# The tile order of a fused attention and convolution kernel, planned with other durations for GpSimd and with two more tile pairs on VectorE

## The chip, the core and the metric
One NeuronCore of a Trainium2 chip. The metric is the device time of one launch in microseconds, as the median of several runs. TensorE (PE) multiplies matrices into PSUM, ScalarE (ACT) and VectorE (DVE) read PSUM, GpSimd (POOL) works on SBUF alone, and SyncE (SP) issues most of the DMAs.

## What is computed
Two branches over the same input x = A_q (2048 tokens, 640 channels, bf16) are mixed by a gate per token:

```
g = sigmoid(sum(x * gate_w))
a = x * (causal_conv(kv, ssm_k) + kv * ssm_D)        # kv = shift4(A_k) * A_v, convolution by FFT of 4096
b = softmax((x @ wq) @ (x @ wk).T / sqrt(20)) @ (x @ wv) @ wo   # 32 heads of 20, one shared k and v
out = g * a + (1 - g) * b
```

The attention has 32 heads over 2048 x 2048 scores, 134 million exponentials. That is the bulk of the work off TensorE. The convolution is done with discrete Fourier transforms as matmuls: spectra of kv and of ssm_k, a complex product of the spectra, and an inverse.

## The kernel before
The attention goes by groups of four heads and 512 queries: 8 head groups x 4 query blocks are 32 groups, counted 0 to 31 (`G`). A group has 16 steps `j` of 128 keys; at each step the four heads give four score tiles of 128 keys x 512 queries, one PSUM bank each. The last group is cut into three stages of 256, 128 and 128 queries, so that the end drains quickly.

Most score tiles are made by TensorE (line 1445), turned into weights by ScalarE (line 1480), and multiplied with the values by TensorE (line 1554). ScalarE takes them in units of three tiles (tile ETA, 1536 columns) and two tiles (ETB, 1024 columns) in turn, over five banks.

For some steps two of the four tiles, a pair, don't go to ScalarE. The table `DVE_J` (line 724) lists for each group the steps with such a pair; `stream` (line 1389 on) takes those tiles out of ScalarE's list and packs the rest into units. For a pair VectorE copies each score tile from one of the two side banks to SBUF (line 1527, dW), then computes the exponential by a cubic in three instructions of 1024 columns (lines 1546, 1547 and 1549; dX, dX, ETd). TensorE then multiplies ETd with the values. There are four ETd buffers, two dW and one dX.

The sum over the keys of a group stands in bank 6. VectorE copies it out when the group closes (line 1635, acc); TensorE can't close a group before all of its pairs have been multiplied in. GpSimd then divides by the row sums (line 1652).

The convolution's matmuls (lines 1821, 1882, 1951) run on TensorE between the score and value matmuls, over the same two side banks, which VectorE empties (lines 1894, 1897, 1901, 1903). Its complex product runs on GpSimd, in `mac`: for each of 40 blocks four products, two sums and two last steps, each of 256 columns (lines 1915 to 1930).

The order of all instructions on all engines is planned when the kernel is built. `Scheduler` steps a clock of each engine forward with an assumed cost for each instruction and picks the next one by readiness, priority and due time (`pick`, `pick_pe`, `pool_may`, `place`); the lists come out fixed, with semaphores between the engines. The planner holds that a VectorE instruction marked `port` (the three wide ones of a pair among them) and a GpSimd instruction exclude each other:

```
if op.port and e == "dve":
    op.end = max(start, self.pool_until - PORTP) + op.cost
elif e == "pool":
    op.end = max(start, self.port_until - PORTD) + op.cost
```

`c_pool(n)` is 0.3 + 0.00168 n us, so `c_pool(256) - 0.045` is 0.685. Where TensorE has nothing to do, the planner puts in matmuls with zeros (line 2045).

Of the kernel before, what the change touches and what calls it, by code (L numbers as in the profile page):

```python
# [7 lines left out]
ALU = mybir.AluOpType  # L8
# [712 lines left out]
TABT = 8.0  # L721
TABR = 12.5
STAGES = ((0, 256, 6), (256, 128, 5), (384, 128, 6))
DVE_J = ((), (3, 7), (2, 4, 7, 8, 11), (1, 4, 14), (1, 3, 13), (1, 7, 8, 11), (1, 2, 6, 9), (9, 13), (1, 4, 5, 6, 10, 14), (1, 4, 11), (2, 7, 9), (1, 4, 7, 14), (1, 2, 5, 6, 11), (2, 3, 8, 10), (2, 5, 6, 8), (2, 5, 6, 13), (1, 2, 5), (7, 10, 11, 13), (1, 2, 5, 12), (1, 3, 8, 13), (1, 8, 11), (1, 7, 8, 14), (3, 4, 12), (3, 9, 10, 14), (4, 9, 14), (3, 10), (2, 3, 6, 11, 13, 14), (1, 2, 9, 11), (2, 3, 6), (1, 2, 5, 6, 9), (1, 2, 9, 10, 13), (2, 5))
KIND = {}
SCALE = float(DH) ** -0.5
CK = SCALE * LOG2E * 128.0
# [34 lines left out]
def c_pool(n):  # L762
    return 0.3 + 1.68e-3 * n
# [6 lines left out]
class Kernel:  # L770
# [618 lines left out]
    def stream(self):  # L1389
# [4 lines left out]
        for G in range(LASTG + len(STAGES)):  # L1394
            for j in range(NSC if G < LASTG else NSC * STAGES[G - LASTG][1] // 512):
                mine = order
                if G <= LASTG and j in DVE_J[G]:
                    mine, rest = order[:2], order[2:]
# [11 lines left out]
    def attention(self):  # L1410
# [148 lines left out]
        def PV(G, j, rs, more=False):  # L1559
# [19 lines left out]
            if j == 0 and G <= LASTG:  # L1579
                for jd in DVE_J[G]:  # L1580
                    pe = self.ndexp % NED
# [326 lines left out]
    def mac(self, c, fc, p, prio):  # L1908

        T = self.T  # L1910
        X, K, P = T[f"X{p}"], T[f"K{p}"], T["Pp"]
        AB = T[f"AB{c % 2}"]

        def tt(out, a, b, alu, reads, writes, n, cost=None):
            f = lambda e: e.tensor_tensor(out, a, b, alu)  # L1915
            self.pool(f, reads, writes, cost or c_pool(n) - 0.045, prio=prio, port=True, name="mac")

        sh = [128, 2, 2, CW]
        sl = 2 + (NF * c + fc) % NP1
        both = slice(1, sl + 1, sl - 1)  # L1920
        for h, o in ((1, 0), (0, 1)):
            for x in range(2):
                tt(P[:, o, x, :, :], X[:, x, :].unsqueeze(1).to_broadcast([128, 2, CW]), K[:, h, :, :], ALU.mult,
                   [("X", p), ("K", p)], [("Pp", o)], 256)
        for x in range(2):
            tt(P[:, sl, x, :, :], P[:, sl, x, :, :], P[:, 0, x, :, :], ALU.add, [("Pp", sl), ("Pp", 0)], [("Pp", sl)], 256, 0.73)
        rd = [("Pp", 1), ("Pp", sl)]
        ab = [("AB%d" % (c % 2), fc)]
        tt(AB[:, fc, :, 0, :], P[:, both, 0, 0, :], P[:, both, 1, 1, :], ALU.subtract, rd, ab, 256)
        tt(AB[:, fc, :, 1, :], P[:, both, 0, 1, :], P[:, both, 1, 0, :], ALU.add, rd, ab, 256)  # L1930
        if fc == 0:

            for x in range(2):
                self.dve(lambda e, x=x: e.tensor_scalar(AB[0:1, fc, :, x, :], P[0:1, both, x, x, :], 0.5, None, ALU.mult), rd, ab, 0.19,
                         prio=prio, port=True, name="row0")
# [169 lines left out]
```

## Time and profile before
| | |
|---|---|
| median of 3 runs | 847.73 us (847.66 to 847.99) |
| the profiled execution | 848.0 us, of which the span from first to last instruction is 846.1 |
| ScalarE busy | 835.8 us, 99% |
| TensorE busy | 824.6 us, 97% |
| VectorE busy | 779.6 us, 92% |
| GpSimd busy | 328.6 us, 39% |
| granted TensorE clock | 1.0 throughout |

Durations of neighbouring instructions on ScalarE, VectorE and GpSimd overlap in the records, since one begins before the last results of the one before have landed. What an instruction costs its engine is read from start to start in a stretch without idle time, not from its duration.

### The profile page before, as it was taken

Reading aid. Unit: us, or ns where it says so; the run is one execution under the profiler, and the core shown is the slowest. Engines: PE = TensorE matmul, PEld = TensorE weight load, DVE = VectorE, ACT = ScalarE, POOL = GpSimd, SP = SyncE. Lnnn points to the kernel's source line nnn. Section 1 sums busy time; section 2 is a strip of 40 time slices with the busy share of each in tenths; the row PEclk is TensorE's granted clock in tenths of the full one; section 3 lists DMA queues with packets and bytes.
Section 4 is the critical chain, followed back from the end, with each engine's and each line's share of the span. In section 5 each row is a group of like instructions: output and inputs, shape, how many; then the busy total and the mean of one; then the engine's idle time right before and its main releaser. Section 6 shows DMA issues by size and latency. Waiting matters only on the chain.

```text
span 846.1 us, 18750 instructions
## 1 busy us (share of the span) xinstructions
PE 824.6 (97%) x7934; PEld 346.5 (41%) x7934; DVE 779.6 (92%) x1057; ACT 835.8 (99%) x748; POOL 328.6 (39%) x418
## 2 busy tenths in 40 slices
PE   8999999999999999999999999999999999999997
PEld 4234433444334444434434344444444443433334
DVE  7788999999999999999999979999989978999995
ACT  8999999999999999999999999999999999999997
POOL 3246102644555344444432653345555444301010
PEclk9999999999999999999999999999999999999999
DMA  7740022001220000200012010000200000422011
GB/s 209 188 114 14 15 57 71 21 14 16 63 59 21 14 17 12 46 20 22 15 37 54 23 44 21 17 7 19 45 21 21 14 2 15 115 69 69 32 41 43
DMA packets 55764, 36.31 MB, mean 43 GB/s; under 512 B 33059, under 2 KB 51712, under 8 KB 55680
## 3 DMA queue, kind: packets, MB, share of 16 engines
q1 hardware_dynamic: 55104, 34.90, 15.6%
q8 instruction: 62, 1.02, 0.5%
q10 hardware_dynamic: 576, 0.22, 0.1%
q14 instruction: 22, 0.18, 0.1%
HBM read 20.31 MB, written 8.51 MB: 34 GB/s over the span
## 4 chain that ended last, share of the span: by engine, by line
ACT 86%; PE 7%; DVE 5%; DMA 1%; SPq 0%; issue 0%
ACT ETA L1480 51%; ACT ETB L1480 35%; PE ps L1445 2%; PE ps L1882 2%; PE ps L1554 1%; DVE dW L1527 1%; DVE dX L1546 1%; DVE dX L1547 1%; DVE ETd L1549 1%; PE ps L1951 1%; DMA xn<-in_A_q_dram 1%; PE ps L1347 0%; PE ps L2045 0%; SPq L795 0%; PE ps L1176 0%
## 5 line engine op out<-in xcount | busy, mean ns | idle before, releaser
L1480 ACT ACTIVATE ETA<-ps 128x1536 bf16<-128x1536 f32 x364 | 573.8, 1576 | 0.8 <-PE ps L1445 0.6
L1480 ACT ACTIVATE ETB<-ps 128x1024 bf16<-128x1024 f32 x363 | 419.6, 1156 | 0.0
L1445 PE MATMUL ps<-qT,kT 32*128 32x512 bf16 (+2 forms) x2176 | 298.5, 371 | 11.1 <-ACT ETA L1480 5.2
L1527 DVE COPY dW<-ps 128x512 f32<-128x512 f32 x230 | 157.0, 684 | 21.9 <-PE ps L1445 19.8
L1915 POOL TENSOR_TENSOR Pp<-X,K 128x256 f32<-128x256 bf16 x160 | 120.0, 758 | 147.3 <-DVE ETd L1549 42.0
L1445 PEld LDWEIGHTS ps<-qT,kT 32*128 32x128 bf16 x2176 | 77.0, 91 | 227.5 <-ACT ETB L1480 111.0
L1554 PE MATMUL ps<-ETA,vaug 128*32 128x512 bf16 (+2 forms) x1168 | 152.8, 370 | 0.0
L1549 DVE SCALAR_TENSOR_TENSOR ETd<-dX,dW 128x1024 int16<-128x1024 f32 x115 | 151.2, 1315 | 0.5
L1547 DVE SCALAR_TENSOR_TENSOR dX<-dX,dW 128x1024 f32<-128x1024 f32 x115 | 149.0, 1296 | 0.6
L1546 DVE SCALAR_TENSOR_TENSOR dX<-dW 128x1024 f32<-128x1024 uint16 x115 | 148.3, 1289 | 1.3
L1554 PE MATMUL ps<-ETB,vaug 128*32 128x512 bf16 (+2 forms) x774 | 146.9, 371 | 0.8 <-ACT ETA L1480 0.7
L1951 PE MATMUL ps<-AB,Tcs 128*128 128x256 bf16 x600 | 90.2, 275 | 0.1
L1882 PE MATMUL ps<-ssm_kT,Tcs 128*128 128x256 bf16 x600 | 90.1, 275 | 0.0
L1882 PE MATMUL ps<-kv,Tcs 128*128 128x256 bf16 x600 | 87.7, 275 | 1.1 <-DVE dW L1527 1.0
L1915 POOL TENSOR_TENSOR AB<-Pp 128x256 bf16<-128x256 f32 x80 | 58.2, 727 | 77.0 <-DVE dX L1546 24.8
L1915 POOL TENSOR_TENSOR Pp<-Pp 128x256 f32<-128x256 f32 x80 | 60.9, 761 | 56.1 <-DVE dX L1547 26.2
L1652 POOL TENSOR_TENSOR oTn<-acc,rbc 128x512 bf16<-128x512 f32 x24 | 40.9, 1703 | 78.1 <-DVE xT L1359 29.2
L1951 PEld LDWEIGHTS ps<-AB,Tcs 128*128 128x128 bf16 x600 | 50.8, 98 | 35.9 <-issue 29.3
L1882 PEld LDWEIGHTS ps<-kv,Tcs 128*128 128x128 bf16 x600 | 49.1, 97 | 39.0 <-issue 25.5
L1882 PEld LDWEIGHTS ps<-ssm_kT,Tcs 128*128 128x128 bf16 x600 | 50.4, 98 | 35.1 <-issue 25.5
L2045 PE MATMUL ps<-Tcs,zeros 128*32 128x512 bf16 (+1 forms) x740 | 62.8, 381 | 1.2 <-DVE acc L1635 1.1
L1652 POOL TENSOR_TENSOR oT<-acc,rbc 128x512 bf16<-128x512 f32 x7 | 10.7, 1532 | 89.4 <-DVE outsb L1984 33.3
(174 smaller groups left out, 644.0 us busy)
## 6 DMA issues: line engine op xcount, KB each, us to landing
rbc<-scr_d SPq DMA_DIRECT2D x31, 256.0 KB
scr_o<-oTn SPq DMA_DIRECT2D x24, 128.0 KB, 1.7
kv<-in_A_v_dram SPq DMA_DIRECT2D x4, 640.0 KB
out_dram<-outsb SPq DMA_DIRECT2D x15, 160.0 KB
xn<-in_A_q_dram SPq DMA_DIRECT2D x3, 640.0 KB
scr_q<-xT SPq DMA_DIRECT2D x15, 128.0 KB, 1.8
qT<-scr_q SPq DMA_DIRECT2D x12, 160.0 KB
oTp<-scr_o SPq DMA_DIRECT2D x12, 160.0 KB, 3.0
```

What stands on the lines that cost most here:

```text
L1445: return e.matmul(self.bank(bk, n, n * t), T["kT0" if first(G, jt) else "kT4"][32 * r:32 * r + 32, 128 * jt:128 * jt + 128], T[k][32 * r:3 ...
L1480: op("act", lambda e: e.activation(et(n)[:, 0:w], self.ps[:, lo:lo + w], ACT.Exp, scale=OCT, bias=-K0 * OCT), [("ps", base[n % 2] + k) for ...
L1527: self.evac(gr, "dve", lambda e, bk, c=c: e.tensor_copy(W[:, c], self.bank(bk)), (), [kW], n).due = G
L1546: V(lambda e: e.scalar_tensor_tensor(X, w, DP, w, ALU.add, ALU.mult), [kW], ["dX"], c_dve(1024), **k).due = G
L1547: self.mid = V(lambda e: e.scalar_tensor_tensor(X, X, DQ, w, ALU.add, ALU.mult), [kW, "dX"], ["dX"], c_dve(1024), **k)
L1549: V(lambda e: e.scalar_tensor_tensor(E, X, DA, W, ALU.mult, ALU.add), [kW, "dX"], [("ETd", pe, 0), ("ETd", pe, 1)], c_dve(1024), **k).due = G
L1554: return op("pe", lambda e: e.matmul(self.bank(b, n)[32 * r:32 * r + 32, :], T[va][:, j, :], src, start=(j == 0 or cut and j == 4 * EARLY) ...
L1652: self.pool(lambda e: e.tensor_tensor(out, T["acc"][:, :], T["rbc"][:, :], ALU.mult), ["acc", "rbc"], [key], 1.27, prio=p, port=True, name ...
L1882: self.mm(gr, lambda e, bk, lhs=lhs, rhs=rhs, comp=comp, n=n: e.matmul(self.bank(bk, 256, 256 * comp), lhs, rhs, start=(n == 0), stop=(n = ...
L1915: f = lambda e: e.tensor_tensor(out, a, b, alu)
L1951: self.mm(gr, lambda e, bk, lhs=lhs, fc=fc, comp=comp, h=h: e.matmul(self.bank(bk, 256, 256 * h), lhs, AB[:, fc, :, comp, :], start=(fc == ...
L2045: sch.filler, *sch.filler2 = ([[lambda e, r=r, st=st, b=b, n=n: e.matmul(self.bank(b, n)[32 * r:32 * r + 32, :], self.T["zeros"][:, 0:32], ...
```

## The change
Two things are changed. `DVE_J` is a new table: 117 pairs in place of 115, and most steps are other ones. And in `mac` the planner's costs of GpSimd's 256-column instructions are 0.63 us for a product (0.685 before), 0.68 for a sum (0.73 before) and 0.685 for a last step (as before). No instruction on GpSimd is added, removed or altered; the costs are used by the planner alone, and so change the order.

```diff
-DVE_J = ((), (3, 7), (2, 4, 7, 8, 11), (1, 4, 14), (1, 3, 13), (1, 7, 8, 11), (1, 2, 6, 9), (9, 13), (1, 4, 5, 6, 10, 14), (1, 4, 11), (2, 7, 9), (1, 4, 7, 14), (1, 2, 5, 6, 11), (2, 3, 8, 10), (2, 5, 6, 8), (2, 5, 6, 13), (1, 2, 5), (7, 10, 11, 13), (1, 2, 5, 12), (1, 3, 8, 13), (1, 8, 11), (1, 7, 8, 14), (3, 4, 12), (3, 9, 10, 14), (4, 9, 14), (3, 10), (2, 3, 6, 11, 13, 14), (1, 2, 9, 11), (2, 3, 6), (1, 2, 5, 6, 9), (1, 2, 9, 10, 13), (2, 5))
+DVE_J = ((), (1, 11), (5, 10, 11, 14), (2, 8, 13, 14), (4, 7, 9), (3, 11, 14), (1, 2, 3, 7), (7, 8), (2, 7, 9, 12, 14), (2, 4, 10, 13, 14), (1, 7, 8, 12), (2, 7, 14), (4, 8, 10, 14), (2, 8, 11), (3, 5, 6, 8, 9, 12), (1, 3, 4), (5, 10, 12), (1, 7, 9, 13), (1, 2, 4, 14), (2, 6, 9, 14), (8, 12, 13, 14), (3, 4, 7), (3, 4, 8, 12), (3, 4, 9, 13), (1, 2, 8, 10), (1, 8, 10, 14), (4, 9, 12, 14), (1, 6, 8, 11, 13), (5, 9), (1, 3, 4, 8, 10, 11), (1, 3, 13, 14), (1, 2, 6))
...
-            self.pool(f, reads, writes, cost or c_pool(n) - 0.045, prio=prio, port=True, name="mac")
+            self.pool(f, reads, writes, cost or 0.63, prio=prio, port=True, name="mac")
...
-            tt(P[:, sl, x, :, :], P[:, sl, x, :, :], P[:, 0, x, :, :], ALU.add, [("Pp", sl), ("Pp", 0)], [("Pp", sl)], 256, 0.73)
+            tt(P[:, sl, x, :, :], P[:, sl, x, :, :], P[:, 0, x, :, :], ALU.add, [("Pp", sl), ("Pp", 0)], [("Pp", sl)], 256, 0.68)
...
-        tt(AB[:, fc, :, 0, :], P[:, both, 0, 0, :], P[:, both, 1, 1, :], ALU.subtract, rd, ab, 256)
-        tt(AB[:, fc, :, 1, :], P[:, both, 0, 1, :], P[:, both, 1, 0, :], ALU.add, rd, ab, 256)
+        tt(AB[:, fc, :, 0, :], P[:, both, 0, 0, :], P[:, both, 1, 1, :], ALU.subtract, rd, ab, 256, 0.685)
+        tt(AB[:, fc, :, 1, :], P[:, both, 0, 1, :], P[:, both, 1, 0, :], ALU.add, rd, ab, 256, 0.685)
```

## Rows read from the trace of the kernel before
The windows of rows 5 from 612 us on end where VectorE copies out the sums of groups 23 to 27.

**Rows 1.** Page, busy us, share and instructions of each engine.
```profile
PE 824.6 (97%) x7934; PEld 346.5 (41%) x7934; DVE 779.6 (92%) x1057; ACT 835.8 (99%) x748; POOL 328.6 (39%) x418
```

**Rows 2.** Timeline of ScalarE: start us, us, engine, line, operation, tiles.
```profile
16.39 1.45 ACT L1480 ACTIVATE ETA<-ps 128x1536 bf16<-128x1536 f32 x1
...
34.81 1.60 ACT L1480 ACTIVATE ETA<-ps 128x1536 bf16<-128x1536 f32 x1
36.14 1.18 ACT L1480 ACTIVATE ETB<-ps 128x1024 bf16<-128x1024 f32 x1
37.04 1.62 ACT L1480 ACTIVATE ETA<-ps 128x1536 bf16<-128x1536 f32 x1
...
838.96 1.70 ACT L1480 ACTIVATE ETA<-ps 128x1536 bf16<-128x1536 f32 x1
```

**Rows 3.** Page, costliest groups: the exponentials; busy us, mean ns, idle before.
```profile
L1480 ACT ACTIVATE ETA<-ps 128x1536 bf16<-128x1536 f32 x364 | 573.8, 1576 | 0.8 <-PE ps L1445 0.6
L1480 ACT ACTIVATE ETB<-ps 128x1024 bf16<-128x1024 f32 x363 | 419.6, 1156 | 0.0
```

**Rows 4.** Timeline around a stall of ScalarE; idle before and releaser in brackets.
```profile
248.83 1.14 ACT L1480 ACTIVATE ETB<-ps 128x1024 bf16<-128x1024 f32 x1
...
249.64 0.28 PE L1882 MATMUL ps<-kv,Tcs 128*128 128x256 bf16 x1 [0.70 <-DVE dW L1527]
...
250.34 1.45 ACT L1480 ACTIVATE ETA<-ps 128x1536 bf16<-128x1536 f32 x1 [0.38 <-PE ps L1445]
```

**Rows 5.** Windows: length; busy PE, PEld, DVE, ACT, POOL; clock, DMA.
```profile
150.00:250.00 100.00, 97.22 (x869) 38.86 (x866) 98.08 (x139) 99.96 (x89) 50.29 (x62) 1.00 0.16 36
...
612.00:638.70 26.70, 26.61 (x242) 11.49 (x241) 23.31 (x33) 26.70 (x25) 13.56 (x20) 1.00 0.06 17
638.70:664.50 25.80, 25.66 (x248) 10.58 (x247) 23.86 (x31) 25.80 (x24) 13.51 (x19) 1.00 0.06 17
664.50:691.50 27.00, 27.00 (x252) 11.79 (x252) 21.27 (x27) 27.00 (x25) 14.46 (x21) 1.00 0.04 12
691.50:715.40 23.90, 23.44 (x231) 9.74 (x230) 21.90 (x25) 23.90 (x22) 9.36 (x13) 1.00 0.04 12
715.40:740.20 24.80, 24.06 (x229) 9.59 (x228) 22.92 (x27) 24.80 (x23) 8.84 (x13) 1.00 0.40 99
```

**Rows 6.** Waits of VectorE from 612 to 740.2: us, times, longest.
```profile
DVE dW L1527 <- PE ps L1445: 10.8, 12, 2.7
```

**Rows 7.** Timeline of VectorE while GpSimd is still.
```profile
107.86 1.21 DVE L1547 SCALAR_TENSOR_TENSOR dX<-dX,dW 128x1024 f32<-128x1024 f32 x1
109.00 0.68 DVE L1527 COPY dW<-ps 128x512 f32<-128x512 f32 x1
109.60 0.68 DVE L1825 TENSOR_TENSOR kv<-ps,kv 128x512 bf16<-128x512 f32 x1
```

**Rows 8.** Page, costliest groups: the wide instructions of the pairs.
```profile
L1549 DVE SCALAR_TENSOR_TENSOR ETd<-dX,dW 128x1024 int16<-128x1024 f32 x115 | 151.2, 1315 | 0.5
L1547 DVE SCALAR_TENSOR_TENSOR dX<-dX,dW 128x1024 f32<-128x1024 f32 x115 | 149.0, 1296 | 0.6
L1546 DVE SCALAR_TENSOR_TENSOR dX<-dW 128x1024 f32<-128x1024 uint16 x115 | 148.3, 1289 | 1.3
```

**Rows 9.** Windows from 0 of line 1549 alone, the last step of a pair.
```profile
0.00:691.50 691.50, 121.97 (x92) 1.00 0.16 41
...
0.00:740.20 740.20, 133.08 (x100) 1.00 0.16 42
```

**Rows 10.** Timeline of GpSimd in a run of products and sums.
```profile
354.36 0.67 POOL L1915 TENSOR_TENSOR Pp<-X,K 128x256 f32<-128x256 bf16 x1
354.99 0.73 POOL L1915 TENSOR_TENSOR Pp<-Pp 128x256 f32<-128x256 f32 x1
```

**Rows 11.** Page, costliest groups: score matmuls, and matmuls with zeros.
```profile
L1445 PE MATMUL ps<-qT,kT 32*128 32x512 bf16 (+2 forms) x2176 | 298.5, 371 | 11.1 <-ACT ETA L1480 5.2
...
L2045 PE MATMUL ps<-Tcs,zeros 128*32 128x512 bf16 (+1 forms) x740 | 62.8, 381 | 1.2 <-DVE acc L1635 1.1
```

## The prediction
> **What bounds the kernel now.** The first view is the page's line of busy times [rows 1]: ScalarE is busy 835.8 of 846.1 us, TensorE 824.6, VectorE 779.6, GpSimd 328.6. Three engines are nearly full, so the busy share alone doesn't name the bound. The second view is ScalarE's own order in time [rows 2]. An exponential over three tiles starts at 34.81, the next over two tiles at 36.14, the next over three at 37.04: each starts where the one before lets go, and five tiles cost 2.23 us (1.33 + 0.90). The first of these instructions starts at 16.39 and the last at 838.96; in between lie 363 such pairs of instructions (364 of three tiles, 363 of two [rows 3]). 363 x 2.23 is 809.5, the stretch is 822.6: ScalarE does nothing else for 97% of the span and loses only some 13 us in it, spread thin. So the time is set by how many tiles ScalarE has to do, plus these 13 us.
>
> The third view shows how one of the larger losses arises [rows 4]: a two-tile exponential starts at 248.83, the next instruction only at 250.34, that is 1.51 after it and not 0.90. ScalarE waited for a score matmul. TensorE, which runs its list in order, stood 0.70 us in front of a spectrum matmul whose bank VectorE had not yet emptied. A late VectorE reaches ScalarE through TensorE's order; the price here was 0.61 us.
>
> The fourth view is VectorE by stretch [rows 5]. From 150 to 250 us it is busy 98.08 of 100: no room for another pair. From 612.00 to 740.20 it idles 3.39 + 1.94 + 5.73 + 2.00 + 1.88 = 14.9 us, and of its idle time there 10.8 us, in 12 waits, is spent in front of the copy that opens a pair, until TensorE has made the scores [rows 6].
>
> **The change, part by part.** *Fewer tiles on ScalarE.* Each pair takes two score tiles from ScalarE to VectorE. The table of pairs sums to 117 and not 115, so ScalarE has 1814 tiles in place of 1818. 1818 is 363 x 5 + 3; 1814 is 362 x 5 + 4, which ends with a three-tile and a one-tile instruction. By [rows 2] a tile is the difference of the two kinds, 1.33 - 0.90 = 0.43, and the fixed part 0.90 - 2 x 0.43 = 0.04. The stream loses one round of 2.23 and gains a one-tile instruction of 0.43 + 0.04 = 0.47 behind the last three-tile one: -1.76 us. All of it is on the path that sets the end.
>
> *More work on VectorE.* A pair is two copies and three 1024-column instructions. From start to start a copy takes 0.60 (109.00 to 109.60) and a wide one 1.14 (107.86 to 109.00) [rows 7]: 2 x 0.60 + 3 x 1.14 = 4.62 us, 9.24 for two pairs. To that comes what the wide ones lose to GpSimd: their means are 1289, 1296 and 1315 ns [rows 8] against 1.21 where GpSimd is still [rows 7], so 0.27 us a pair and 0.5 for two. The sum is 9.8 us of VectorE. On the path it is nothing if idle time takes it. Where does it fall? Added up group by group, the new table stands at or below the old through group 23, but for one pair after group 10 (85 in both after 23), then at 93 against 90 after group 25, 102 against 100 after group 27, and 117 against 115 at the end. VectorE works a little ahead of its table: when groups 25 and 27 close, at 691.50 and 740.20, it has finished 92 and 100 pairs [rows 9], so it must have one more and two more by then. So the full stretch gets no more work, and the two pairs have to be absorbed between about 612 and 740 us, where the idle time is 14.9 us against the 9.8 needed. It fits, with 5 us left in 128. I take 0 for this edit. The bounds: at worst only the idle time that isn't a wait for scores can be used, 14.9 - 10.8 = 4.1 us, and 9.8 - 4.1 = 5.7 us come late; at best a VectorE whose pairs sit better removes a few stalls, below.
>
> What [rows 8] show of GpSimd is that the wide instructions last longer on average than alone, while none is stopped for good. The Trainium skill (SBUF — State Buffer, "Who interferes with whom") says that VectorE instructions with two SBUF inputs and GpSimd instructions that read SBUF exclude each other through a lock, the later one blocked fully until the first ends. If each of the six added wide instructions met a whole GpSimd instruction of 0.67 us [rows 10], that would be 4.0 us in place of 0.5, and the sum 13.3 of the 14.9: still room, but next to none. The trace agrees that they hinder each other, but its 0.27 us a pair is a small share of that.
>
> *The planner's new GpSimd durations.* 160 products are entered at 0.63 and not 0.685, 80 sums at 0.68 and not 0.73; the 80 last steps keep 0.685. The trace has one product starting at 354.36 and the next instruction at 354.99, 0.63 later [rows 10], so the new figure is what the chip does. GpSimd's instructions are the same, so nothing is saved there directly: the plan held 160 x 0.055 + 80 x 0.05 = 12.8 us of GpSimd time that the chip never used, and let VectorE wait for part of it. That is why the chip's VectorE runs ahead of its list and stands in front of scores. The correction lets the plan spend this. What it may cost is the spare time itself: plan and chip now agree, and whatever the plan still has wrong meets less cover.
>
> *TensorE.* The number of score and value matmuls stays. Four tiles change from the shared score rounds to single ones that ride beside others; at worst each stands alone for 0.37 us [rows 11], 1.5 in all. I take 0: TensorE's list contains 62.8 us of dummy matmuls that are put in only where there is nothing else to do [rows 11].
>
> *All pairs placed anew.* Which of ScalarE's stalls go and which come cannot be read from the diff. The 13 us are the frame: none can gain more. Single large ones like that of [rows 4] cost 0.61; I take no change, and a spread of 1.2 us to either side, two of them.
>
> Sum: -1.76. The profiled execution took 848.0 us (span 846.1 and 1.9 around it), which makes 846.2; the median of the runs is 847.73, 0.27 less, so 846.0.
>
> **The rivals.**
> 1. *The stalls shrink too.* For it: orders now planned with durations that the chip keeps, so fewer waits in the wrong place. Against: the old figures erred on the long side, and an engine that is early makes few stalls. With a sixth of the 13 us gone as well, -1.76 - 2.1: 843.9.
> 2. *The saving is eaten.* Two or three new stalls of 0.61, since VectorE keeps 5 us of spare time where it had 14.9: 846.0 + 1.5 = 847.5, no change. For it: in the stretch with 98% busy [rows 5] lies the stall of [rows 4].
> 3. *VectorE becomes the bound in groups 24 to 27.* It cannot use its waits for scores, because these come when TensorE's list has them, and TensorE's list is tied to ScalarE. Then 5.7 us come late at the sums that close those groups, ScalarE waits for TensorE behind them, and the time is 847.73 + 5.7 - 1.76 = 851.7. It decides as soon as less than 9.8 - 1.76 = 8.0 us of the 14.9 can be filled. Against it: the waits exist because the old table had no earlier pair to give there, and the new one has.
> 4. *The change doesn't do what it says*: the order that the corrected durations give is, on the chip, no better matched than the old one, and ScalarE waits for TensorE as much longer (1.8 us of 13 would do) as it computes less: 847.7. Against it: the new durations are the chip's own.
>
> **How the numbers follow.** The forecast of 846.0 (its own range 844.8 to 847.2) has a chance of 0.48, rival 1 0.20, rivals 2 and 4 together 0.20, rival 3 0.12. What a measurement can tell from no change is about 0.2%, 1.7 us: under 846.0 counts as faster, over 849.4 as slower. The forecast lies right at that edge. Just over half of its chance (0.28) and all of rival 1 are faster: 0.48. The rest of the forecast (0.20) and rivals 2 and 4 are the same: 0.40. Rival 3 is slower: 0.12. The range reaches from a little beyond rival 1, 843.3, to part of the way into rival 3, 849.2; about 1 in 10 is left out on either side.
>
> **What would show it.** In the trace after: 363 three-tile and 362 two-tile exponentials with a one-tile one at the end, ScalarE's stretch from first to last shorter by 0.9 us (the last one starts a whole round earlier and one three-tile instruction later), and the same 1.33 and 0.90 between starts. VectorE's idle time from 612 to 740 falls from 14.9 to about 5, its waits for scores with it, while 150 to 250 stays near 98%. GpSimd's product still takes 0.63. Rival 1 would show as a stretch shortened by more than that; rival 2 as some further gaps of half a microsecond on ScalarE after 640 us; rival 3 as gaps on ScalarE near 715 and 740 released by TensorE behind VectorE. The forecast is wrong if ScalarE's losses move from 13 us by more than 1.2.

## The result, and the profile after

The kernel after takes 850.82 us (median of 6 runs, 850.58 to 851.75), the kernel before 847.86 beside it: a ratio of 1.0035, 95% interval [1.0022, 1.0048]. It is slower by 3 us, where 1.7 faster was forecast, and 1.6 us above the range. Run again (e11) it took 850.65, a ratio of 1.0034 [1.0022, 1.0047].

The page of after: span, busy times, the chain that ended last by engine, and the costliest groups that answer to [rows 3, 8] and to the complex product on GpSimd.
```profile
span 849.2 us, 18930 instructions
...
PE 824.7 (97%) x8007; PEld 348.9 (41%) x8018; DVE 789.1 (93%) x1067; ACT 836.8 (99%) x747; POOL 342.3 (40%) x418
...
ACT 51%; PE 25%; DVE 21%; issue 1%; DMA 1%; POOL 0%; SPq 0%
...
L1915 POOL TENSOR_TENSOR Pp<-X,K 128x256 f32<-128x256 bf16 x160 | 117.8, 743 | 147.6 <-DVE dX L1547 41.1
...
L1915 POOL TENSOR_TENSOR AB<-Pp 128x256 bf16<-128x256 f32 x80 | 69.8, 872 | 84.9 <-DVE dX L1546 33.7
...
L1915 POOL TENSOR_TENSOR Pp<-Pp 128x256 f32<-128x256 f32 x80 | 65.0, 812 | 40.6 <-DVE dX L1546 18.4
```

The same lines of before's page, as far as they weren't shown.
```profile
ACT 86%; PE 7%; DVE 5%; DMA 1%; SPq 0%; issue 0%
...
L1915 POOL TENSOR_TENSOR Pp<-X,K 128x256 f32<-128x256 bf16 x160 | 120.0, 758 | 147.3 <-DVE ETd L1549 42.0
...
L1915 POOL TENSOR_TENSOR AB<-Pp 128x256 bf16<-128x256 f32 x80 | 58.2, 727 | 77.0 <-DVE dX L1546 24.8
L1915 POOL TENSOR_TENSOR Pp<-Pp 128x256 f32<-128x256 f32 x80 | 60.9, 761 | 56.1 <-DVE dX L1547 26.2
```
Two things stand out. The chain runs through TensorE and VectorE for 46%, where it had run through ScalarE for 86%. And GpSimd, whose 320 instructions of the product are the same ones, is busy 13.7 us longer than in [rows 1]: the last steps take 872 ns on average and not 727, the sums 812 and not 761, while the products take 743 and not 758.

The timeline of ScalarE in after, first and last exponentials; they answer to [rows 2].
```profile
16.30 1.45 ACT L1480 ACTIVATE ETA<-ps 128x1536 bf16<-128x1536 f32 x1
...
840.96 1.51 ACT L1480 ACTIVATE ETA<-ps 128x1536 bf16<-128x1536 f32 x1
842.29 0.67 ACT L1480 ACTIVATE ETB<-ps 128x512 bf16<-128x512 f32 x1
```
From these starts the loss of ScalarE can be counted, which is used from here on: the time from the first start to the last, less what the rounds between them take at the smallest round that the traces show, 1.33 + 0.903 = 2.233 us. With 115 pairs that floor is 363 x 2.233 = 810.6, with 117 it is 362 x 2.233 + 1.33 = 809.7. Before loses 838.96 - 16.39 - 810.6 = 12.0 us, after 842.29 - 16.30 - 809.7 = 16.3. So the last start comes 3.33 us later: 4.3 from more loss, less 0.9 of floor and less 0.1 because the first start is earlier. Behind it the end takes 849.2 - 842.29 = 6.9 us, and 7.1 in before. The whole result is in the 4.3 us. They lie in many small gaps, none over 0.56 us: 2.7 of them from 150 to 450 us, 2.1 from 600 to 750, 0.7 after 800, and a little less loss than before elsewhere.

The windows of VectorE's full stretch and of the one with idle time, in after (columns as in [rows 5]), and then VectorE's waits from 612 to 740.
```profile
150.00:250.00 100.00, 97.81 (x878) 41.17 (x879) 96.94 (x135) 99.51 (x88) 51.10 (x64) 1.00 0.13 37
612.00:740.00 128.00, 123.84 (x1185) 52.27 (x1187) 119.86 (x141) 127.72 (x114) 65.24 (x75) 1.00 0.13 35
```
```profile
DVE dW L1527 <- PE ps L1445: 5.3, 6, 1.3
```
VectorE's idle time there falls from 14.9 us [rows 5] to 128 - 119.9 = 8.1 and its waits for scores from 10.8 [rows 6] to 5.3: the two pairs did go mostly where the prediction put them. Half of the new loss arises elsewhere.

### The profile page after: what moved, and what is told of

Its sections match the earlier page's. It is cut to its first block, busy times and chain, and to the rows that moved or that the text cites. A ratio compares the mean times of both kernels' runs of the same rounds, so it can differ in the third digit from the quotient of the medians.

```text
span 849.2 us, 18930 instructions
## 1 busy us (share of the span) xinstructions
PE 824.7 (97%) x8007; PEld 348.9 (41%) x8018; DVE 789.1 (93%) x1067; ACT 836.8 (99%) x747; POOL 342.3 (40%) x418
## 4 chain that ended last, share of the span: by engine, by line
ACT 51%; PE 25%; DVE 21%; issue 1%; DMA 1%; POOL 0%; SPq 0%
ACT ETA L1480 31%; ACT ETB L1480 20%; PE ps L1445 8%; PE ps L1882 6%; DVE dX L1546 5%; DVE dW L1527 4%; PE ps L1554 4%; DVE dX L1547 4%; DVE ETd L1549 4%; PE ps L1951 3%; PE ps L2045 1%; DVE Pp L1897 1%; DMA xn<-in_A_q_dram 1%; DVE acc L1635 1%; PE ps L1694 1%
## 5 line engine op out<-in xcount | busy, mean ns | idle before, releaser
L1480 ACT ACTIVATE ETA<-ps 128x1536 bf16<-128x1536 f32 x363 | 556.6, 1533 | 2.1 <-PE ps L1445 1.1
L1480 ACT ACTIVATE ETB<-ps 128x1024 bf16<-128x1024 f32 x363 | 403.6, 1112 | 0.2 <-PE ps L1445 0.2
L1527 DVE COPY dW<-ps 128x512 f32<-128x512 f32 x234 | 159.8, 683 | 19.5 <-PE ps L1445 18.2
L1915 POOL TENSOR_TENSOR Pp<-X,K 128x256 f32<-128x256 bf16 x160 | 117.8, 743 | 147.6 <-DVE dX L1547 41.1
L1546 DVE SCALAR_TENSOR_TENSOR dX<-dW 128x1024 f32<-128x1024 uint16 x117 | 154.2, 1318 | 1.4
L1547 DVE SCALAR_TENSOR_TENSOR dX<-dX,dW 128x1024 f32<-128x1024 f32 x117 | 151.8, 1298 | 0.6
L1915 POOL TENSOR_TENSOR AB<-Pp 128x256 bf16<-128x256 f32 x80 | 69.8, 872 | 84.9 <-DVE dX L1546 33.7
L1882 PE MATMUL ps<-ssm_kT,Tcs 128*128 128x256 bf16 x600 | 87.8, 274 | 0.4 <-DVE kv L1961 0.2
L1915 POOL TENSOR_TENSOR Pp<-Pp 128x256 f32<-128x256 f32 x80 | 65.0, 812 | 40.6 <-DVE dX L1546 18.4
L2045 PE MATMUL ps<-Tcs,zeros 128*32 128x512 bf16 (+2 forms) x824 | 70.7, 380 | 1.1 <-DVE acc L1635 0.8
```

The costliest lines, as they stand in the source:

```text
L1480: op("act", lambda e: e.activation(et(n)[:, 0:w], self.ps[:, lo:lo + w], ACT.Exp, scale=OCT, bias=-K0 * OCT), [("ps", base[n % 2] + k) for ...
L1527: self.evac(gr, "dve", lambda e, bk, c=c: e.tensor_copy(W[:, c], self.bank(bk)), (), [kW], n).due = G
L1546: V(lambda e: e.scalar_tensor_tensor(X, w, DP, w, ALU.add, ALU.mult), [kW], ["dX"], c_dve(1024), **k).due = G
L1547: self.mid = V(lambda e: e.scalar_tensor_tensor(X, X, DQ, w, ALU.add, ALU.mult), [kW, "dX"], ["dX"], c_dve(1024), **k)
L1882: self.mm(gr, lambda e, bk, lhs=lhs, rhs=rhs, comp=comp, n=n: e.matmul(self.bank(bk, 256, 256 * comp), lhs, rhs, start=(n == 0), stop=(n = ...
L2045: sch.filler, *sch.filler2 = ([[lambda e, r=r, st=st, b=b, n=n: e.matmul(self.bank(b, n)[32 * r:32 * r + 32, :], self.T["zeros"][:, 0:32], ...
```

## What happens on GpSimd

The timelines of VectorE and of GpSimd in after, around 650 us.
```profile
648.86 1.27 DVE L1549 SCALAR_TENSOR_TENSOR ETd<-dX,dW 128x1024 int16<-128x1024 f32 x1
650.05 0.68 DVE L1527 COPY dW<-ps 128x512 f32<-128x512 f32 x1
650.65 0.24 DVE L1645 RECIPROCAL rcp<-den 128x16 f32<-128x16 f32 x1
650.81 1.18 DVE L1546 SCALAR_TENSOR_TENSOR dX<-dW 128x1024 f32<-128x1024 uint16 x1
652.06 0.69 DVE L1527 COPY dW<-ps 128x512 f32<-128x512 f32 x1
```
```profile
648.32 0.72 POOL L1915 TENSOR_TENSOR Pp<-Pp 128x256 f32<-128x256 f32 x1
650.21 0.67 POOL L1915 TENSOR_TENSOR Pp<-X,K 128x256 f32<-128x256 bf16 x1 [1.16 <-DVE ETd L1549]
650.84 1.74 POOL L1915 TENSOR_TENSOR Pp<-Pp 128x256 f32<-128x256 f32 x1
```
GpSimd's product waits for the wide instruction that started at 648.86. That one's record ends at 650.13; VectorE has begun its next at 650.05, and GpSimd begins at 650.21: 0.08 us after the record's end, 0.16 after VectorE's next start. After has 163 such waits, and the 0.08 is 78 to 81 ns in all of them; in before it is so in 171 of 173. The product then takes its 0.63, so the sum comes at 650.84. But a wide instruction has begun at 650.81. The sum, 0.03 us too late, lasts 1.74 us where its like took 0.72 at 648.32. A race lost by 0.03 us holds GpSimd for a whole microsecond. Of the 320 instructions those over 0.8 us are 14 in before and 30 in after. In 24 of the 30 the record of GpSimd's instruction begins between 0.25 us behind and 0.05 us ahead of the start of a wide one; in before it is so in 8 of 14.

How a long GpSimd instruction reaches ScalarE is seen in the chain of waits of after (start, us, what).
```profile
157.48 1.15 DVE dX L1546
158.62 0.07 issue
158.69 2.24 POOL AB L1915
160.93 0.02 issue
160.96 0.28 DVE AB L1934
161.24 1.14 DVE ETd L1549
162.38 0.04 issue
162.43 0.39 PE ps L1554 x2
...
164.32 1.45 ACT ETA L1480
```
A last step of the product takes 2.24 us; VectorE's small instruction on its result waits for it, the last step of a pair waits behind that in VectorE's order, TensorE's value matmul waits for the pair, and ScalarE for the scores behind it. But this last step lost no race of the kind above, as the timelines of VectorE and GpSimd show.
```profile
158.53 0.67 DVE L1365 TENSOR_SCALAR cr<-ps 32x512 int16<-32x512 int32 x1
159.13 1.20 DVE L1547 SCALAR_TENSOR_TENSOR dX<-dX,dW 128x1024 f32<-128x1024 f32 x1
```
```profile
158.69 2.23 POOL L1915 TENSOR_TENSOR AB<-Pp 128x256 bf16<-128x256 f32 x1 [3.85 <-DVE dX L1546]
```
It begins 0.44 us ahead of the wide instruction and 0.16 behind an instruction of line 1365, which the planner doesn't mark `port`. Two of after's 30 long ones stand behind that line, and three of before's 14, so this kind was there before the change.

The planner doesn't know GpSimd's start. Where `place` ties a GpSimd instruction to a VectorE one (`op.deps.add(d[-2])`), the plan lets it begin as soon as the other ends. From a product's start it then lets VectorE's next wide instruction begin after the product's cost less `PORTP` (0.05): 0.685 - 0.05 = 0.635 us in before, 0.63 - 0.05 = 0.58 in after. On the chip the wide one, counted back 1.13 us from VectorE's next start, effectively begins 0.54 after the product's start (the median of 44 such cases in after); that is within 0.58, but the product may itself start 0.16 late, and 0.54 + 0.16 = 0.70 is more than either. By that reading the old surplus was no idle time: it paid for most of a start that the plan doesn't have. This is the theory (A). Its rivals: (B) the two pairs' load leaves too little spare time, whatever the durations; (C) these are just two placings of the pairs, and any other would differ as much.

## The experiments

All in one table first; "allowed" is the plan's cost of a product less `PORTP`. Medians are over all runs of a kernel, each ratio against runs of before beside it; the loss and the number of long instructions come from one profiled run each. Those of e1 and e7 were 0.4 and 0.7 us faster than their medians, those of e10 and e12 1.1 slower; the two of after's order (after and e11) lose 16.3 and 16.0. So differences in loss of some tenths carry little.

| kernel | pairs | allowed, us | median us | ratio to before [95%] | loss us | GpSimd over 0.8 us |
|---|---|---|---|---|---|---|
| before | 115 | 0.635 | 847.86 | | 12.0 | 14 |
| after | 117 | 0.58 | 850.82 | 1.0035 [1.0022, 1.0048] | 16.3 | 30 |
| e1 | 115 | 0.58 | 849.61 | 1.002 [1.0011, 1.0029] | 13.7 | 14 |
| e2 | 115, other table | 0.635 | 847.83 | 1.0 [0.9991, 1.0008] | 11.8 | 13 |
| e7 | 117, other table | 0.58 | 849.47 | 1.0017 [1.0008, 1.0027] | 14.7 | 16 |
| e8 | 117, other table | 0.62 | 848.2 | 1.0 [0.9991, 1.0009] | 14.0 | 15 |
| e9 | 117, other table | 0.635 | 850.62 | 1.003 [1.0018, 1.0041] | 13.4 | 26 |
| e10 | 116 | 0.66 | 848.18 | 1.0003 [0.9994, 1.0012] | 12.3 | 10 |
| e11 | after again | 0.58 | 850.65 | 1.0034 [1.0022, 1.0047] | 16.0 | 30 |
| e12 | 115, other table | 0.66 | 847.36 | 0.999 [0.9981, 0.9999] | 10.9 | 4 |
| e3 | order of after, product left out | | 845.51 | 0.9971 [0.996, 0.9982] | 10.9 | |
| e4 | order of before, product left out | | 846.53 | 0.9982 [0.9973, 0.9991] | 10.6 | |
| e5 | order of after, 232 columns | | 846.33 | 0.9979 [0.997, 0.9988] | 11.5 | |
| e6 | order of before, 232 columns | | 846.74 | 0.9984 [0.9976, 0.9993] | 10.8 | |

**e1, the durations alone, and e2, a new placing alone.** e1 is after with 115 pairs, before's table through group 6 and then placed for the new durations. e2 is before with another table of 115.
```diff
-DVE_J = ((), (1, 11), (5, 10, 11, 14), (2, 8, 13, 14), (4, 7, 9), (3, 11, 14),
...
+DVE_J = ((), (3, 7), (2, 4, 7, 8, 11), (1, 4, 14), (1, 3, 13), (1, 7, 8, 11),
...
```
```diff
-DVE_J = ((), (3, 7), (2, 4, 7, 8, 11), (1, 4, 14), (1, 3, 13), (1, 7, 8, 11),
...
+DVE_J = ((), (3, 5), (3, 4, 8, 13), (5, 7, 14), (2, 7, 8, 9, 12, 13), (),
...
```


> The new GpSimd costs alone: 115 pairs as before, and the table of before kept through group 6 and refitted after it only so that the planner, with the new costs, again sees ScalarE without stalls. Theory A (the padding of the old costs had paid for what the planner leaves out when the port passes between VectorE and GpSimd, so VectorE and GpSimd now come late against the list): slower than before, 849.5 to 852 us, with more GpSimd instructions of over 0.8 us than the 14 among the 320 of line 1915 before. Theory B (the two added pairs are too much for VectorE, the costs are harmless): 847.9 within 1 us.

> The old costs and 115 pairs, but another table, found from a scrambled start so that the planner sees ScalarE without stalls. Theory A and theory B: 847.9 within 1 us. Theory C (any table other than the old one loses a few us on the chip, whatever the costs): 849.5 us or more.

e1 takes 849.61 and loses 13.7 us, e2 847.83 and 11.8. The new durations alone, with no pair more, cost 1.6 us; a wholly new table for the old durations costs nothing. That is for A and against B and C as the only cause, though each stands on one table, and e1's table differs from before's behind group 6. One thing was missed: e1 has no more GpSimd instructions over 0.8 us than before, so the long ones alone are not the measure of what a short plan costs. Nor is the chain. By engine, on the pages of e1 and then of e2, it turns away from ScalarE in both, and e2 lost nothing:
```profile
ACT 62%; DVE 22%; PE 14%; issue 1%; DMA 1%; SPq 0%
...
ACT 67%; DVE 16%; PE 14%; DMA 1%; issue 1%; SPq 0%; POOL 0%
```

**e3 and e4, no contention.** The orders of after and of before, with each of the 320 instructions as a write alone.
```diff
-            f = lambda e: e.tensor_tensor(out, a, b, alu)
+            f = lambda e: e.memset(out, 0.0)
```


> The changed kernel with its order untouched, but the 320 instructions of GpSimd's complex product replaced by writes of zero that read nothing (the product is left out). Theory A: GpSimd no longer holds VectorE or is held, the losses of ScalarE fall from 16 to 12 us or less and the time to 846.5 or less. Theory C (the order on TensorE and in the banks is worse in itself): the time stays near 850 us.

> The same in the kernel before. Theory A: it gains less than the changed kernel does, under 2 us, to 846 to 847.5 us, since its plan had cover; the changed kernel without the product is then at or below this one. Theory C: the gap of 3 us between the two remains.

The wide instructions and the products of e3, on its page:
```profile
L1547 DVE SCALAR_TENSOR_TENSOR dX<-dX,dW 128x1024 f32<-128x1024 f32 x117 | 144.3, 1234 | 0.7
L1549 DVE SCALAR_TENSOR_TENSOR ETd<-dX,dW 128x1024 int16<-128x1024 f32 x117 | 144.4, 1234 | 0.2
...
L1546 DVE SCALAR_TENSOR_TENSOR dX<-dW 128x1024 f32<-128x1024 uint16 x117 | 142.8, 1221 | 1.4
L1915 POOL MEMSET Pp<- 128x256 f32 x240 | 73.7, 311 | 283.4 <-DVE dX L1546 76.5
```
The wide ones take 1.22 to 1.23 us, close to the 1.21 of [rows 7]. After's order is now the faster, 845.51 against 846.53, and the two lose about the same (10.9 and 10.6). So the order of after is not bad in itself: 1.0 of the forecast 1.76 us shows. What undoes it is GpSimd: of the 4.3 us that after loses more than before, 0.3 are left. The edit takes away two things at once, the contention and more than half of each instruction's length (311 ns); e5 separates them.

The Trainium skill (SBUF — State Buffer, "Who interferes with whom") says that a VectorE instruction with two SBUF inputs contends with a GpSimd instruction that reads SBUF and not with one that only writes it. The trace of e3 agrees: 311 ns for each write, and wide instructions nearly as short as alone. It also says ("SBUF: two separate sides") that whichever of the two starts first gets the shared ports for its whole instruction and blocks the other; the sum at 650.84 above, 1.74 us for 0.72, agrees with that. The other way the trace shows less than a whole one: the wide instruction effectively begins 0.54 us into a product that takes 0.63.

**e5 and e6, the contention kept, GpSimd slightly shorter.** Each of the 320 instructions has 232 columns in place of 256, in both orders; the inverse transform reads columns that are written, and VectorE's small instruction on the product is cut to 64 columns.
```diff
+            h = CW - 12
+            out, a, b = out[..., 0:h], a[..., 0:h], b[..., 0:h]
             f = lambda e: e.tensor_tensor(out, a, b, alu)
...
```


> The changed kernel, its order untouched; GpSimd's 320 instructions work on 232 of the 256 columns (the rest of the product is left out, and the inverse transform reads 64 columns of it twice), so that each is some 0.05 us shorter than the plan has it: the padding put back, on the chip and not in the plan. Theory A: ScalarE's losses fall from 16 to 12 or 13 us and the time to 846 to 848 us. Theory B (too many pairs): 320 x 0.05 is only 16 us less of GpSimd, VectorE has as many pairs as before, the time stays at 850 or above.

> The same shortening in the kernel before, as the control. Theory A: its plan has the padding already, so more of it gains under 1 us: 847 to 848 us.

The GpSimd groups of e5, on its page:
```profile
L1917 POOL TENSOR_TENSOR Pp<-X,K 128x232 f32<-128x232 bf16 x160 | 106.1, 669 | 156.9 <-DVE dX L1547 43.1
...
L1917 POOL TENSOR_TENSOR AB<-Pp 128x232 bf16<-128x232 f32 x80 | 60.5, 756 | 91.3 <-DVE dX L1546 37.7
L1917 POOL TENSOR_TENSOR Pp<-Pp 128x232 f32<-128x232 f32 x80 | 59.0, 737 | 44.2 <-DVE dX L1546 19.9
```
The means fall by 743 - 669 = 74 ns, 116 and 75, which is some 0.04 us of the instructions' own length (a product that isn't held records 0.63 and not 0.67) and, for the rest, shorter holds. That gives after 4.5 us (850.82 to 846.33) and before 1.3 (848.0, measured beside it, to 846.74, where under 1 was expected), and turns the order of the two round by 0.4 us. The order stays as planned with the new durations, GpSimd is given back about what the plan had taken away, and the new order loses 11.5 and not 16.3. With e3 this shows where the loss sits: between GpSimd and VectorE, in the new order. It doesn't part A from B, because VectorE is relieved too: its busy time falls from 789.1 to 779.7 us in e5 and from 779.6 to 770.9 in e6.

**e7, a second table of 117** for the new durations.
```diff
-DVE_J = ((), (1, 11), (5, 10, 11, 14), (2, 8, 13, 14), (4, 7, 9), (3, 11, 14),
...
+DVE_J = ((), (3, 11), (1, 5, 11), (4, 9, 10, 12, 14), (5, 12), (1, 2, 14),
...
```


> The new costs and 117 pairs with another table, found from a scrambled start so that the planner sees ScalarE without stalls. Theory A: it loses like the changed kernel, 849.5 to 852 us. Theory C (the table of the change was bad luck): 847 us or less.

849.47, 1.3 us less than after, with 16 long GpSimd instructions and not 30. So C holds a part: between two tables of 117 lie 1.3 us. Both are slower than before. But 1.45 of e7's 14.7 us of loss lie in one stall at 350 us. ScalarE there, and then the matmul ahead of its scores:
```profile
348.84 1.05 ACT L1480 ACTIVATE ETB<-ps 128x1024 bf16<-128x1024 f32 x1
351.19 1.45 ACT L1480 ACTIVATE ETA<-ps 128x1536 bf16<-128x1536 f32 x1 [1.30 <-PE ps L1445]
```
```profile
350.43 0.28 PE L1882 MATMUL ps<-ssm_kT,Tcs 128*128 128x256 bf16 x1 [1.30 <-DMA ssm_kT<-in_A_ssm_k_dram]
```
TensorE waited for a load of ssm_k, not for VectorE or GpSimd. Without this stall e7 loses 13.3, 3.0 less than after and no more than e1 with its 115 pairs.

**e8, 117 pairs and a hand-over nearer to the chip's.** `PORTP` is what the plan takes off after GpSimd, `PORTD` what it takes off after VectorE.
```diff
-PORTP = 0.05
-PORTD = 0.14
+PORTP = 0.01
+PORTD = 0.055
...
```


> The new costs and 117 pairs, but the planner's two allowances for passing the port are set by the traces as well: after a product VectorE's wide instruction begins 0.62 us after GpSimd's start, which with a cost of 0.63 is an allowance of 0.01 and not 0.05; and a held GpSimd instruction gets 0.055 and not 0.14 of overlap. Table refitted. Theory A: ScalarE's losses are back at 12 or 13 us and the saving of the two pairs shows: 845.5 to 847 us, below the kernel before. Theory B: 850 us or more, since VectorE has the same pairs.

A correction to that text: the 0.62 us that it gives from GpSimd's start to VectorE's wide instruction was counted back from the recorded end; from start to start, as planned, it is 0.54. So the edit didn't set the chip's hand-over; its table apart, it gave 0.04 us of padding after GpSimd and, with `PORTD`, 0.085 after VectorE. The result is 848.2, level with before, 1.3 us below e7 and 2.6 below after, but not below before as A had expected; the loss is 14.0, not 12 or 13. And the table is a third one of 117: two tables alone differ by 1.3 us, so how much of the gain is the padding's isn't shown.

**e9, the two pairs alone:** before's durations, a table of 117.
```diff
-DVE_J = ((), (3, 7), (2, 4, 7, 8, 11), (1, 4, 14), (1, 3, 13), (1, 7, 8, 11),
...
+DVE_J = ((), (8, 10), (9, 10, 11, 13), (6, 9, 10), (3, 5, 7, 12), (3, 4, 14),
...
```


> The old costs with 117 pairs, table refitted (the planner sees ScalarE without large stalls, but with the old costs it leaves VectorE's last work some 2 us later at the end than in the kernel before). Theory A: ScalarE's stream loses 12 to 13 us as before, its last instruction starts 1 to 2 us earlier than in the kernel before, and the time is 847 to 848.5 us because of the end. Theory B: the stream loses 14 us or more, and the time is 849.5 us or above.

850.62: A had expected 847 to 848.5 us and a last start 1 to 2 us earlier, and missed. The loss is 13.4, 1.4 above before, and the last start, at 839.18, is 0.2 us later than before's, so the stream gains nothing; then the end takes 848.9 - 839.2 = 9.7 us, 2.8 more than in after. VectorE's last two instructions in e9:
```profile
843.54 0.54 DVE L1748 SCALAR_TENSOR_TENSOR outsb<-ps,omgf,part 128x320 bf16<-128x320 f32 x1
845.71 0.88 DVE L1782 SCALAR_TENSOR_TENSOR outsb<-ps,omgf,part 128x640 bf16<-128x640 f32 x1 [1.63 <-PE ps L1724]
```
The last output, which starts 3.7 us after the last exponential in after (846.02), starts 6.5 us after it here, after 1.63 us of waiting for TensorE's output matmul. So e9 bears on B only up to 839: two pairs more cost 1.4 us of loss with the old durations, where they save 0.9 of floor. That is again one table. The late end is this plan's own.

**e10, 116 pairs, and e12, 115, padded.** The products' 0.63 stays and the plan adds 0.03 where it took 0.05 off; after VectorE it takes 0.055 off and not 0.14, as in e8. In e12 this holds only from the start of the main stream on.
```diff
-                op.end = max(start, self.pool_until - PORTP) + op.cost
+                op.end = max(start, self.pool_until - (-0.03 if self.main_started else PORTP)) + op.cost
...
-                op.end = max(start, self.port_until - PORTD) + op.cost
+                op.end = max(start, self.port_until - (0.055 if self.main_started else PORTD)) + op.cost
...
```


> 116 pairs, the new costs, and the two allowances set to pay for GpSimd's start as well: VectorE's wide instruction is planned to begin 0.03 us after GpSimd's cost is over (not 0.05 before), a held GpSimd instruction gets 0.055. Table refitted. Theory A: losses of 12 to 13 us and, with two tiles less, 846.5 to 848 us, at or below the kernel before. Theory B (each pair beyond 115 costs more than it saves): 848.5 us or more.

> 115 pairs, the new costs, and the allowances of the padded run with 116 pairs, but only from the first exponential on, so that the start of the kernel is planned as before. Table refitted. Theory A (what loses time is a plan that lets VectorE go on earlier than GpSimd's late start allows): ScalarE's stream loses 11 to 11.5 us, less than the 12 of the kernel before with the same number of tiles, and the time is 846.5 to 847.5 us, faster than both kernels. If losses stay at 12 or above with the hand-over paid for, something else makes them, and the time is 848 or more.

e10 loses 12.3 us, of which 1.3 in one stall at 24.2 us, and its first exponential starts at 18.40, 2 us late; it comes out level with before, between what A (848 at most) and B (848.5 or more) had expected. e12 loses least of all kernels with the whole product, 10.9, has 4 long GpSimd instructions, and its chain goes through ScalarE again; its time is where A expected it. Its page:
```profile
ACT 89%; PE 6%; DVE 3%; DMA 1%; SPq 0%; issue 0%
...
L1915 POOL TENSOR_TENSOR Pp<-X,K 128x256 f32<-128x256 bf16 x160 | 108.0, 683 | 172.4 <-DVE dX L1547 51.4
...
L1915 POOL TENSOR_TENSOR AB<-Pp 128x256 bf16<-128x256 f32 x80 | 59.2, 740 | 83.7 <-DVE dX L1546 32.8
L1915 POOL TENSOR_TENSOR Pp<-Pp 128x256 f32<-128x256 f32 x80 | 59.1, 739 | 55.0 <-DVE ETd L1549 25.6
```
Its median of 847.36 is below both kernels, but by 0.1% to before, and its runs spread from 846.1 to 848.63; the profiled one, 848.45, has its first exponential at 17.87, 1.5 us later than before's. TensorE's waits for the load of x, ahead of that start, are 3.1 us in it and 2.1 in before; whether the late start belongs to its order was not settled.

**e11, after again,** unchanged.

> The changed kernel once more, beside the others on one chip: 850.8 us, with ScalarE's losses at 16 us.

850.65, loss 16.0, again 30 long GpSimd instructions: the slowness belongs to the order, not to a run.

**Read together.** What is shown: the new order loses 4.3 us more than the old one as long as GpSimd and VectorE hold each other up, 0.7 more with GpSimd's instructions slightly shorter, and 0.3 more without the product. How the 4.3 divide is less sure, because every kernel with other durations or pairs has a table of its own. With 115 pairs the loss is 13.7 us where the plan allows 0.58, 12.0 and 11.8 at 0.635, and 10.9 at 0.66 (there with the other change, after VectorE, as well): less allowance, more loss, which is for A. With 117 it is 16.3 and 14.7 (13.3 without the load stall) at 0.58, 14.0 at 0.62, 13.4 at 0.635: apart from after itself there is no clear trend. Two pairs more lose 1.4 us more at 0.635, and 2.6 or 1.0 more at 0.58, or nothing if the load stall is left out (B); 0.9 would be saved on the floor. And between two tables with the same pairs and durations, after and e7, lie 1.6 us of loss, or 3.0 (C). So the kernels with 115 pairs speak for A, each of the three may have a part, and this table's own share may be the largest.

## Why the prediction was wrong

*The step that failed* is "All pairs placed anew": "I take no change, and a spread of 1.2 us to either side". The losses rose by 4.3 us, of which e3 and e4 leave 0.3 and e5 and e6 0.7: what the prediction put at nothing is VectorE and GpSimd holding each other up in the new order. It rested on a sentence of the step on the planner's durations, "the plan held 160 x 0.055 + 80 x 0.05 = 12.8 us of GpSimd time that the chip never used", and on "plan and chip now agree". The pitch of 0.63 is right by itself [rows 10], but it was read inside a run of GpSimd's instructions. By A, a cost in the plan has to cover the first one too, which starts 0.16 us after VectorE has gone on; e1 puts the price of the shorter durations at 1.7 us of loss with one table, and the rest came with the pairs and with this table. The prediction asked what a product takes and not what passes between VectorE's end and VectorE's next chance. The trace of before showed it: the same 78 to 81 ns stand there behind 171 of 173 such waits.

*Fewer tiles on ScalarE.* Right: the stream ends with a one-tile instruction at 842.29, and the floor is lower by the 0.9 us named. e3 against e4 shows 1.0 us of the 1.76 on the chip.

*More work on VectorE.* Half right. The pairs went into the idle time from 612 to 740, which fell to 8.1 us and not to 5. But taking 0 for them isn't borne out: with the old durations 117 pairs lose 1.4 us more (e9 against before), and with the new ones after loses 2.6 more than e1, e7 1.0 more or, without its load stall, nothing. The full stretch wasn't spared either: 150 to 450 us lost 2.7 us more in after, though the table asks for no more pairs there.

*TensorE.* Nothing contradicts the 0; no run tested it alone.

*The rivals.* Rival 3 named 851.7, near the result, for another cause. From 700 to 725 us after loses 0.1 us, less than before's 0.4; only 0.4 us at 669 and 0.4 at 742 lie near where a group's sum is copied out. Rival 4 had the right mechanism, an order "no better matched than the old one", at less than half of its size: 1.8 us of loss where 4.3 came. "An engine that is early makes few stalls", said against rival 1, was the right observation, and it should have weighed for a slower kernel.

*Still open:* how the loss divides between durations, pairs and table, and between starts that are late in themselves, lost races and less spare time (e1 has the loss without more long instructions), and whether 117 pairs could gain on before with an allowance of 0.66. Several tables at each allowance would answer the first, a plan of 117 at 0.66 the last; neither was run.

## What to carry to other kernels

A planner's duration that looks too long may be paying for a latency that the plan doesn't have: before trimming it, compare hand-overs from the one engine's end to the other's next start, not only the pitch within a run of one engine's instructions. Where two engines exclude each other, being late by a few hundredths of a microsecond can cost a whole instruction of the other (1.02 us at 650.84), so a margin in the plan may be worth its time. One planned order stands for itself alone: two tables with the same pairs and durations differed by 1.3 us here, so an effect of that size needs several of them. To test an order against its plan, change the chip's durations under the unchanged order (e5) as well as the plan under the unchanged kernel.

## What the hardware showed unexpectedly

- A GpSimd instruction of the product that waits for a VectorE one starts 0.08 us after that one's recorded end, which is 0.16 after VectorE's next start where VectorE went straight on: 78 to 81 ns in all 163 waits of after and in 171 of 173 of before.
- A GpSimd instruction that begins while VectorE's line 1365 (32x512, int32 to int16) runs takes 2.08 to 2.34 us when a wide instruction follows within 0.6 us (13 times in the nine traces of kernels with the whole product, e11's apart), and 0.67 to 0.73 when it follows later (9 times). One more began together with the wide one. Why line 1365 does this isn't shown.
- Memsets of GpSimd, 311 ns each, barely lengthen VectorE's wide instructions (1221 to 1234 ns in e3, 1298 to 1318 in after).
- The first exponential of one and the same order started from 16.10 to 16.67 us in its profiled runs (after, e3, e5 and e11), so orders are better compared by the loss between first and last start than by single runs.
